# A 21st turned head, more turned steps in the MLP's middle, and output sums on ScalarE and GpSimd, in an attention and MLP kernel

## Chip, cores and metric

The kernel runs on one core of one Trainium2 chip. The metric is the device time of one execution in microseconds (us); lower is better.

## What is computed

All in float32, with S = 2048 tokens, D = 448, 16 heads of 28 columns that share one key and one value head, and F = 1792:

```python
xn  = layernorm(x)
q   = (xn @ wq) in 16 heads;  k = xn @ wk;  v = xn @ wv
att = softmax(q k^T * 28**-0.5) v, heads joined, @ wo
mlp = gelu(layernorm(xn) @ w1 + b1) @ w2 + b2
out = x + att + mlp
```

## The kernel before

Tokens are cut into 4 chunks of 512 columns (`CW`). A float32 product is made of three single-pass matmuls on a high part and a low part (`xh`, `xl`, `w1h`, `w1l` and so on). There are three stages.

**First stage (to about 65 us).** Norms, projections, `ks` (keys, all 2048 columns), `vs` (values), and queries written to DRAM as `qd`.

**MLP (about 65 to 487 us).** `slot(n)` runs one of 56 pairs (chunk, 128 rows of F): 11 matmuls of the first layer into the one bank `ph` (`mlp1`, L262 to L267), ScalarE and GpSimd work for the gelu, and 12 matmuls of the second layer for the pair of two slots earlier (`mlp2`, L787). Between those 12, `stages` calls jobs by position: `closing` and `middle` are the gelu's second and third part, `texp` is `turned_exp`. The loop over `slot(n)` (from L837) counts the matmuls: with `pace` 21, each matmul adds 21 to `owed`, and whenever a multiple of 46 is passed, one **step** of the attention's preparation is issued, 10.5 per slot. It is of one of two kinds:

- a **max step** (`max_stream`, L668 and L669): one matmul of 128 queries by 512 keys, and a VectorE reduce to the row maximum. A head takes 16. The maxima go into the score matmul as two more rows (`load_max`), so that the exp can be taken with keys on the partitions.
- a **turned step** (`turned_scores`, L704 and L705): the same matmul for a head of `TURNED`, but VectorE scales the scores into the SBUF tile `raw` and takes the maximum on the way. After four steps (one tile of 128 queries, L711 joins the four maxima) two exps of 128x1024 (`turned_exp`, L722) follow on ScalarE, and four DMAs (L725) on SP's queue store the tile in DRAM, turned by blocks. 16 steps make a head. There are two `raw` tiles (`RAWS`), and a step that finds more than two exps queued yields without work.

In a slot up to four turned steps come first (not in the odd slots of the first chunk), then max steps.

**Attention (487 us to the end).** 16 units (chunk c, group g of 4 heads), each of 16 key tiles. A **plain head** takes per key tile one score matmul with keys on the partitions (L1104) and one exp (L1105); a **turned head** has its exps in DRAM, `load_quarters` (L902 on) brings them back by 512 KB DMAs on SP's queue, two per `quarter` tile of six, each behind a one-element VectorE memset that marks the buffer as free (L912), and VectorE transposes 128x1024 of it by 32x32 blocks (`turn_blocks`, L1080). Then four matmuls of 32 columns each add the weighted values (`pv`, L1068). So 16 turned steps take the place of 16 max and 16 score matmuls.

`TURNED` lists the turned heads: head 3 of each unit, and head 2 of units 9, 11, 13 and 15; 20 in all.

The order of the attention is written out by hand: `ORDERS` has one string for each four key tiles (64 of them). `s` is a score, `m` a max step, `t` a turned step, `x` a turned exp, `T` a transpose, a digit that many key tiles of weighted values, `n` a step of the unit's normalization (`norm_jobs`: GpSimd DMAs and multiplications), `e` the next unit's maxima, `o` a step of the output product, `|` the second half. `BANKS` gives the PSUM bank (0 to 6) of each product in that order. What the MLP has not done of the 320 turned and 704 max steps is done here: 128 and 314.

`o_jobs` (L937 on) adds, for each of a chunk's four token tiles, 12 matmuls (L944 to L946) into one bank, and VectorE adds it to the row tile `a` (L948), which goes out. In the attention `loads` is GpSimd's queue, which takes the query and row-sum DMAs.

Of the kernel before, what the change touches and what calls it, by code (L numbers as in the profile page):

```python
# [26 lines left out]
SCALE = DH ** -0.5  # L27
PAIRS = 13
ORDERS = (
    "ssmsmssmmmssmTmssTs|ss",  # L30
    "tss|4TtstssmsstmsmstsssT",
    "Tsxsm|4estssmsmssmtsmsmTss",
    "ssxssTTms5smsmssmmmsms|s",
    "sstssxmTtxm3mmnmsnstTssns|ssms",
    "Tss3|stnnmssmmssmtssTsxss",
    "smT|nssxs6Teststmsmsstssnsnn",
    "TsnssT|mss3tsmsnstsmmsssmmx",
    "sTxsmsnns|s4Tmsmtsssmsnss",
    "nssnT|tsT3sstsstsmmsntsssx",
    "Tst|smsx4nnnTesmsmnsmtssssxss",  # L40
    "ssm4Tsmmssmss|nnstsmTsss",
    "|snTnsnm2ssmmsmssmsssmsmttxT3msm",
    "sstnTs|nssmmsmxT3smsmsnnntsssmm",
    "tmmsxsns|s3TstmesmtsTnssxsnss",
    "n|Tts5nxsmsssmTstmsnmsss1nss",
    "|nmstmtssTmstTsssms4omsmmomsssn",
    "sss|onnmTsmmxn3sTmemnsotssstosss",
    "mmxnT|tss3smsnmnsmmssmssmsTsnmms",
    "sxsm4xTtsnsmm|sssttstsnsxnxsTs",
    "tsnsTs6Ttmsststsossmssso|",  # L50
    "nTs2s|mssmmntsssstttssssm3To",
    "3xnxTsmss|nmsnmTmsnemsssxomsssmsm",
    "|sTssnsnsTsmontsnmmnmtxssts4smsm",
    "|ssmntTsnssTxstmxstm4mtsnsnstsms",
    "sns|xTs5nxesmnmstsssnstmsssT",
    "T|snsnomstsmssstsTttss2sns",
    "|ssmmssmmtxnnm5xTmstssmssnTsss",
    "T|sxsmottnsssmmsmsmxtm3T1msmmtsnnsss",
    "Tn|smnssse2smssmsmsnTsss",
    "sstnx|mx4nTtsmstsssnmmmsssTsns",  # L60
    "TssT3|stssnmmssssxsnss",
    "m|mx3Tstsstsnmmmmmssnm4oooooTmtssnonsmsosmsm",
    "sTn|tmmxT4xsmsmsmssmntsmststnnsss",
    "|smtsmTsm3stemsssmmmsTnmsmsmnss",
    "xTmmn4|ssmssnmmsnnsmtTsssntxsss",
    "ssT5sTTmtsmTnsnmss|s",
    "o|TTs4snsnmmsmnmTsTssmnsmx",
    "T|Tsnsss4essmstTsmTmo",
    "ssntsTsmx4TnnmTsT|sss",
    "sssnmnnmt4tnsstsxmsm|mTnmxossssmnsT",  # L70
    "ns|Toesssnmmststnsnmmntxxtmmm4mmssmmsmsmsT",
    "|ssTssmnnssmmT5mmsstsnstsms",
    "T|mssmtmomsstTsm2sntsmmssstmsxs",
    "T|mnmmT5msmnTTsstnsssss",
    "Tn4sTmssnm|TnsmsnTsss",
    "TTsxs4men|sssnsssTT",
    "sTsnTssTx51snTm|msmss",
    "mmssmsxnmssTssmnn2mnmsmsTstssn|",
    "ss1ssm|tsmnssmttTttsxoxmt4esoosnnmssmmT",
    "ssonssmtT|sn3smmnssmssmnnmTss",  # L80
    "xossxTsmomTt5mos|msnmssmnmsmssss",
    "|sTmTsnTs3msntostsnToss",
    "smsmmnsTTtsnsTsn6|Tss",
    "TstmsnmtnTostsxmsTe7Txnmssm|ts",
    "Tnnssmnosmsmn|TmxxnttTsTosss",
    "s|TTst6tsmmmsnnssmxmsss2sss",
    "TmtststTssts3xnnxmmsssmsmnnmsxsm|s",
    "ssTs3ensnsTssns|ssss",
    "sT3s|nssssTssssn3sns",
    "Ts|snssssT2nnTssT",  # L90
    "TsTsTss2ssnn|Tss",
    "ssss2TsTsooso4TsoT|",
    "sssTssssT|s3TT",
)
BANKS = (
    "0163240516324053126543126043512604352106342510634251063425016324051632450163245013465201345620135640"
    "2135640213546023150426314502631450236451203645102364150236145023641502346510324653102465301425603145"
    "2063145206345120163452061345260314526031456230145632104562314056234105623401526354021635410256431025"
    "6431026540635142063510462504635120641325063412506342105634251064235106425316042530416523041562031465"
    "2103465210346521304652130465132064532104653210463045621340526314052631450264352106435210463521046352"  # L100
    "1064532106453126045132604513624015362453016243501264350126435012645031642501346250143560214365021436"
    "5021436510423651402635401263540126345012506342156043201456320146503421650342165304261354601235406213"
    "5402615324103416520431650234160523416052431605431260541302564325160425361402610523460512346051234061"
    "5342016532401635204165302416530246153206543120643512046351024631052460351420653210465231046532106532"
    "4106532406513245061324506132405163025461302564130526134052164350216043521604351260435612045361240356"
    "1203456102435604132560143520641352601453601245631024651302465132046513204635104635210462315046231506"
    "42351604325610345216304521630452163045216304521630452130452130452130415230415"
)
TURNED = tuple((u, j) for u in range(16) for j in ((3, 2) if u in (9, 11, 13, 15) else (3,)))
RAWS = 2  # L110
GELU = 0.044715, 0.7978845608028654
KEPT = 1, 2, 3
MLP_ORDER = 1, 2, 3, 0
# [5 lines left out]
def block_kernel(ctx, tc, x, wq, wk, wv, wo, w1, b1, w2, b2, out):  # L119
# [4 lines left out]
    def f(t):  # L124
        return t.bitcast(F32)
# [569 lines left out]

    def turned_scores(i):
        for t in range(CT):
            while len(exps) > 2:
                yield
            raw = keep.tile([P, 4, 4, P], F32, name="raw", bufs=RAWS)  # L700
            m3 = keep.tile([P, 8], F32, name="m3", bufs=RAWS)
            for n in range(4):
                sc = mtile([P, CW])
                pe.matmul(sc, q3[i % 2][:, t * P:(t + 1) * P], ks[:, n * CW:(n + 1) * CW], start=True, stop=True)  # L704
                dve.tensor_scalar(raw[:, n].rearrange("p r (b i) -> p b r i", i=32),  # L705
                                  sc.rearrange("p (b r i) -> p b r i", r=4, i=32), SCALE, -3e38,
                                  op0=ALU.mult, op1=ALU.max, accum_out=m3[:, n:n + 1])
                if (t, n) == (0, 3) and 0 < i < len(TURNED) - 1:
                    load_m(*TURNED[i + 1], q3[1 - i % 2])
                if n == 3:  # L710
                    dve.tensor_reduce(m3[:, 4:5], m3[:, 0:4], axis=AX.X, op=ALU.max, negate=True)  # L711
                    exps.extend((TURNED[i], t, raw, m3, h) for h in range(2))
                yield

    stored = {}

    def turned_exp():
        if not exps:
# [23 lines left out]
    def split(c, ft):  # L742
        return c == 0 and ft % 2 == 1
# [53 lines left out]
    def slot(n):  # L797
        nonlocal maxed, ending, later_low
        middle = high = low = none
        closing, ending = ending, none  # L800
        if n < len(mslots):
            if n == 0:
                high, later_low = w2_split(0)
            if n > 1 and split(*mslots[n]):
                high, low = w2_split(n // 2)
                high()
            middle, ending = yield from mlp1(*mslots[n], closing if n == 1 else none)
        if n == 2:
            later_low()
        texp = turned_exp if n < len(mslots) - 1 else none  # L810
        stages = {0: texp, 1: texp, 2: low, 3: closing, 5: middle}
        if n == 0:
            stages = {0: middle, 1: high}
        if n == 1:
            stages = {1: texp, 2: texp, 3: middle}
        if n == 3:
            stages = {0: closing, 1: low, 2: texp, 3: texp, 5: middle}
        if n in norms:
            stages = {4: norms[n], 5: texp, 6: texp, 7: closing, 8: norms[n], 9: middle, 10: low}
        if n >= 2:  # L820
# [16 lines left out]
    for n in range(len(mslots) + 2):  # L837
# [22 lines left out]
        if c == NCH - 1 and 6 <= ft < 12:  # L860
            for i in (2 * ft - 12, 2 * ft - 11):
                q, r = divmod(i, 4)
                nc.sync.dma_start(ahead[q][:, 4 * r:4 * r + 4, :], td[0, 3][q, :, 4 * r:4 * r + 4])
        ts, pace = 0, 21
        if n == 2:
            pace = 20
# [35 lines left out]
    def load_quarters(n):  # L902
        u, q = divmod(n // 2, 4)
        at = slice(8 * (n % 2), 8 * (n % 2) + 8)
        for j in (3, 2):
# [6 lines left out]
            dve.memset(part[0:1, 0, 0:1], 0.0)  # L912
            nc.sync.dma_start(part, td[u, j][q, :, at])

    pool.memset(wor, 0.0)
# [21 lines left out]
    def o_jobs(c, gs, tiles=range(CT)):  # L937
        last = NG - 1 in gs
        for k in tiles:
# [5 lines left out]
                pe.matmul(po, oth[:, ts], wol[:, g, :], start=False, stop=False)  # L945
                pe.matmul(po, otl[:, ts], woh[:, g, :], start=False, stop=(g == gs[-1]))  # L946
            a = rows[c, k]
            dve.tensor_add(a, a, po)  # L948
            if last:
                nc.sync.dma_start(ov[:, CT * c + k, :], a)  # L950
            yield
# [254 lines left out]
```

## Time and profile before

| | us |
|---|---|
| median of 3 runs | 1047.93 |
| lowest, highest | 1047.56, 1048.78 |
| the profiled execution | 1048.25 |
| its span, first to last instruction | 1046.4 |
| MLP up to | about 487 |
| attention from there | about 559 |

The profile is of one execution. Engines are PE (TensorE's matmuls), PEld (its weight loads), DVE (VectorE), ACT (ScalarE), POOL (GpSimd) and SP (SyncE's queue). A row of the timeline has start, length, engine, line and operation; neighbouring equal operations are joined with their count, so the length of a joined row spans all of them. A group row of the page has busy time, mean ns of one, and the idle time before with what ended it. A window row has, for each engine, the busy time and the number of instructions, then the granted clock of TensorE, the DMA engines' share and GB/s. A row of waits has total, number of times and the longest.

### The profile page before, as it was taken

What the parts mean: (1) busy time and instruction counts of PE and PEld (TensorE: products, weight loads), DVE (VectorE), ACT (ScalarE), POOL (GpSimd) and SP (SyncE); (2) the same over time, 40 slices, a digit from 0 to 9 for tenths busy, and PEclk for the clock granted to TensorE, in tenths of its full rate; (3) what the DMA queues carried; (4) which work ended last, traced back from release to release, by engine and by line L of the source; (5) the groups of instructions that cost most, each with busy time, mean ns of one, the idle gap of its engine ahead of it and who ended that gap; (6) DMA issues with size and microseconds to landing.
All of it is one profiled execution on the core that took longest, in us unless ns stands there. A gap on an engine that the chain in (4) does not pass through costs nothing.

```text
span 1046.4 us, 17964 instructions
## 1 busy us (share of the span) xinstructions
PE 1037.4 (99%) x5757; PEld 704.9 (67%) x5757; DVE 935.1 (89%) x1998; ACT 722.8 (69%) x1216; POOL 562.0 (54%) x704
## 2 busy tenths in 40 slices
PE   8999999999999999999999999999999999999998
PEld 8778888888888888886555545655555555455555
DVE  7889999999999999999887988878899999998956
ACT  6765555565566565655899888877877666875892
POOL 6679787678766777875244354234335342441230
PEclk9999999999999999999999999999999999999999
DMA  8866455767776867984789798887889998899892
GB/s 273 252 212 168 120 141 146 186 153 196 194 190 157 205 174 192 265 231 137 217 247 263 219 270 231 254 252 241 245 241 267 308 258 287 269 292 308 265 354 78
DMA packets 234130, 234.33 MB, mean 224 GB/s; under 512 B 19007, under 2 KB 199373, under 8 KB 234037
## 3 DMA queue, kind: packets, MB, share of 16 engines
q1 hardware_dynamic: 221684, 212.45, 69.8%
q0 software_dynamic: 10944, 20.17, 7.5%
q8 instruction: 45, 0.74, 0.3%
q10 hardware_dynamic: 1408, 0.57, 0.2%
q14 instruction: 49, 0.39, 0.1%
HBM read 133.21 MB, written 98.68 MB: 222 GB/s over the span
## 4 chain that ended last, share of the span: by engine, by line
PE 91%; DVE 4%; DMA 3%; issue 1%; ACT 1%; ACTq 0%; DVEq 0%
PE po L1068 19%; PE m L1104 15%; PE m L668 15%; PE m L787 12%; PE ph L262 11%; PE m L704 7%; PE qp L262 3%; DMA quarter<-td 2%; DVE mx L669 2%; PE ph L265 1%; PE ph L267 1%; PE m L944 1%; PE m L946 1%; PE m L945 1%; DVE p L1080 1%
## 5 line engine op out<-in xcount | busy, mean ns | idle before, releaser
L669 DVE TENSOR_REDUCE mx<-m 128x1 f32<-128x512 f32 x704 | 451.8, 682 | 32.3 <-PE m L668 29.7
L1105 ACT ACTIVATE p<-m 128x512 f32<-128x512 f32 x612 | 318.1, 633 | 79.8 <-PE m L1104 78.2
L668 PE MATMUL m<-ks,qm 128*128 128x512 f32 x704 | 268.6, 399 | 1.6 <-DVE mx L669 0.6
L705 DVE TENSOR_SCALAR_CACHE_REDUCE raw<-m 128x512 f32<-128x512 f32 x320 | 212.3, 684 | 22.0 <-PE m L704 18.3
L1104 PE MATMUL m<-xh,ks 128*128 128x512 f32 x704 | 223.6, 406 | 0.0
L1068 PE MATMUL po<-p,vs 128*32 128x512 f32 x1664 | 221.0, 595 | 0.4 <-DVE p L1080 0.4
L722 ACT ACTIVATE raw<-raw,m 128x1024 f32<-128x1024 f32 x160 | 180.1, 1165 | 4.4 <-DVE m L711 4.2
L1104 PEld LDWEIGHTS m<-xh,ks 128*128 128x128 f32 x704 | 127.6, 188 | 68.4 <-issue 15.9
L1080 DVE STREAM_TRANSPOSE p<-quarter 128x1024 f32<-128x1024 f32 x133 | 161.1, 1228 | 7.6 <-DMA quarter<-td 7.2
L668 PEld LDWEIGHTS m<-ks,qm 128*128 128x128 f32 x704 | 131.4, 188 | 45.6 <-issue 7.5
L752 ACT ACTIVATE hx<-ph,b1t 128x512 f32<-128x512 f32 x55 | 37.9, 690 | 150.1 <-PE ph L267 98.7
L1068 PEld LDWEIGHTS po<-p,vs 128*32 128x32 f32 x1664 | 55.6, 109 | 109.2 <-issue 103.1
L704 PE MATMUL m<-ks,q 128*128 128x512 f32 x320 | 125.5, 399 | 0.0
L768 POOL TENSOR_TENSOR hl<-hx,hh 128x512 fp32r<-128x512 f32 x56 | 72.5, 1294 | 32.7 <-ACT hh L766 32.7
L787 PE MATMUL m<-w2h,hl 128*128 128x448 f32 x224 | 81.4, 367 | 0.0
L787 PE MATMUL m<-w2h,hh 128*128 128x448 f32 x224 | 81.3, 366 | 0.0
L787 PE MATMUL m<-w2l,hh 128*128 128x448 f32 x224 | 81.2, 366 | 0.0
L756 POOL TENSOR_TENSOR hz<-hz,hx 128x512 f32<-128x512 f32 x56 | 72.8, 1299 | 4.6
L761 POOL TENSOR_TENSOR hx<-hx,hz 128x512 f32<-128x512 f32 x56 | 72.6, 1297 | 4.7
L704 PEld LDWEIGHTS m<-ks,q 128*128 128x128 f32 x320 | 59.8, 188 | 22.2 <-issue 5.0
L633 POOL DMA_DIRECT2D xh<-qd x60 | 37.5, 626 | 64.7 <-PE m L668 40.8
L1068 PE MATMUL po<-xh,vs 128*32 128x512 f32 x256 | 68.2, 596 | 0.0
(198 smaller groups left out, 1529.6 us busy)
## 6 DMA issues: line engine op xcount, KB each, us to landing
td<-raw SPq DMA_DIRECT2D x320, 256.0 KB
quarter<-td SPq DMA_DIRECT2D x154, 512.0 KB
xh<-qd POOLq DMA_DIRECT2D x44, 168.0 KB, 5.4
qd<-qe SPq DMA_DIRECT2D x24, 256.0 KB
a<-in_A_x_dram SPq DMA_DIRECT2D x24, 224.0 KB
qm<-qd SPq DMA_DIRECT2D x96, 56.0 KB
qm<-qd POOLq DMA_DIRECT2D x80, 56.0 KB, 5.4
ad<-a SPq DMA_DIRECT2D x16, 224.0 KB
```

The lines of the kernel that those rows point to most:

```text
L262: pe.matmul(ps, w, v, start=(n == 0), stop=False)
L668: pe.matmul(pm, qm[:, t * P:(t + 1) * P], ks[:, n * CW:(n + 1) * CW], start=True, stop=True)
L669: dve.tensor_reduce(mx[:, CT * j + t, n:n + 1], pm, axis=AX.X, op=ALU.max)
L704: pe.matmul(sc, q3[i % 2][:, t * P:(t + 1) * P], ks[:, n * CW:(n + 1) * CW], start=True, stop=True)
L705: dve.tensor_scalar(raw[:, n].rearrange("p r (b i) -> p b r i", i=32), sc.rearrange("p (b r i) -> p b r i", r=4, i=32), SCALE, -3e38, op0= ...
L722: act.activation(raw[:, rs], raw[:, rs], AF.Exp, bias=m3[:, 4:5], scale=1.0)
L756: pool.tensor_mul(hz, hz, hx)
L787: pe.matmul(m2[k], h[:, k * P:(k + 1) * P], w[:, ft, :], start=(ft == 0 and i == 0), stop=(ft == NF - 1 and i == 2))
L1068: pe.matmul(po[32 * j:32 * j + 32, :], vs[:, kt, :], ps.pop((u, kt, j)), start=(kt == 0), stop=(kt == NT - 1))
L1080: dve.transpose(p.rearrange("p k (g j) -> p g k j", j=32), part[:, :, 32 * k:32 * k + 64].rearrange("p g (k j) -> p g k j", j=32))
L1104: pe.matmul(s, ks[:, kt * P:(kt + 1) * P], qss[u][:, j, :], start=True, stop=True)
L1105: act.activation(p, s, AF.Exp, scale=SCALE)
```

## The change

- `TURNED`: the second turned head is in units 4, 7, 10, 13 and 15 now; 21 turned heads. `ORDERS` and `BANKS` are written anew for it.
- `MORE = 15, 43`: from slot 15 to slot 43 a third tile for `raw` is taken from the pool `xl_p`; in these slots up to 4, 8, 4 turned steps (by n % 3) come first, up to four exps may be queued, and `mlp2` has two more places (7 and 9) for a turned exp.
- `load_quarters`: the memset only ahead of the first half of a `quarter` tile.
- `o_jobs`: for chunks 0 to 2 ScalarE copies the bank to a new tile `ot` (one buffer), and GpSimd adds it to `a`. The last chunk's sums stay on VectorE.

In the order strings the letters now count: `s` 688 (704 before), `m` 334 (314), `t` 108 (128), `x` 54 (64), `T` 168 (160); weighted sums 254 key tiles in both.

```diff
-TURNED = tuple((u, j) for u in range(16) for j in ((3, 2) if u in (9, 11, 13, 15) else (3,)))
+TURNED = tuple((u, j) for u in range(16) for j in ((3, 2) if u in (4, 7, 10, 13, 15) else (3,)))
 RAWS = 2
+MORE = 15, 43
...
     def turned_scores(i):
         for t in range(CT):
-            while len(exps) > 2:
+            while len(exps) > (4 if third else 2):
                 yield
-            raw = keep.tile([P, 4, 4, P], F32, name="raw", bufs=RAWS)
-            m3 = keep.tile([P, 8], F32, name="m3", bufs=RAWS)
+            turn_of[0] = (turn_of[0] + 1) % 3 if third else 0
+            raw = third[0] if turn_of[0] == 2 else keep.tile([P, 4, 4, P], F32, name="raw", bufs=RAWS)
+            m3 = keep.tile([P, 8], F32, name="m3", bufs=RAWS + 1)
...
-    stored = {}
+    stored, third, turn_of = {}, [], [0]
...
+        if MORE[0] <= n < MORE[1] + 2:
+            for i in (7,9):
+                if i not in stages:
+                    stages[i] = texp
...
+        if n == MORE[0]:
+            third.append(f(xl_p.tile([P, 4, CW], F32R, name="xl")).rearrange("p a (b k) -> p a b k", k=P))
+        if n == MORE[1]:
+            third.clear()
...
+                elif third and ts < (4, 8, 4)[n % 3]:
+                    ts += tq.step()
+                elif third:
+                    maxed += mxs.step()
                 elif ts < 4 and n < len(mslots) - 1 and not split(c, ft):
...
-            dve.memset(part[0:1, 0, 0:1], 0.0)
+            if n % 2 == 0:
+                dve.memset(part[0:1, 0, 0:1], 0.0)
             nc.sync.dma_start(part, td[u, j][q, :, at])
...
             a = rows[c, k]
-            dve.tensor_add(a, a, po)
+            if c < NCH - 1:
+                t = att.tile([P, D], F32, name="ot", bufs=1)
+                act.activation(t, po, AF.Copy)
+                pool.tensor_add(a, a, t)
+            else:
+                dve.tensor_add(a, a, po)
```

Of `ORDERS` every string is new; the 43rd, in unit 10, for one:

```diff
-    "|ssTssmnnssmmT5mmsstsnstsms",
+    "nTmmmsnmnsns4|txTmssmmsostoTTmsn",
```

More of the change, by code (lines that the diff above doesn't have):

```diff
@@ L29 @@
 ORDERS = (
[L30 to L70, printed above, removed]
@@ L71 @@
-    "ns|Toesssnmmststnsnmmntxxtmmm4mmssmmsmsmsT",
-    "|ssTssmnnssmmT5mmsstsnstsms",
[L73 to L93, printed above, removed]
+    "ssmmssmmsmsTmsT|sssss",
+    "|sTs3stsmmsmsssmTtsttsss",
+    "s3esmsmssttms|stTsmxxsmsss4Tm",
+    "sst|sssmTTsxxstssms4tsttsm",
+    "sssssxsmsmm2TmsmtssmnsT|ns",
+    "ssstsns3|mesnnstsmssxsmTTs",
+    "sssTss|4msnstssnxxstssT",
@@ new lines @@
+    "sm5Tsmsstsmnnttss|mssssTs",
+    "sTs2smsnstsmnmsnmsssmssT|",
+    "ssTsn|2mtmssxsnsnsmTmsn2esstns",
+    "nmmtsss|nmssxm23TxnmsmnsmssnmxTsss",
+    "Tsssns4|ssTmssmssmsmns",
+    "ss|Tnnt5Tmnsnmsmnsmsssssss",
+    "|TTmn2mmssmsmmnssssmsnssnnss",
+    "T2n|ttsmsttstTtemnx4xmstsssmsmmsmsss",
+    "snTm|tmxts2mssssnntmssssmsTs",
+    "T|s6snnTTTmsmssmxsss",
+    "TTTsstnT4|1nesmsnmsmsmsnms",
+    "snsmmtTTxsss3nssT|Ts",
+    "sossTssTxT4mssmns|T",
+    "ss1mtssnnmnsmss|smssmtntT3motomsmnTsmn",
@@ new lines @@
+    "TssssntmT5mstsnsmsmm|sssns",
+    "mmnmmos|nsmmxtex2smsmssmnmsmnnsmTsnssTnsm",
+    "sxstxms32TtsmmssstssstnTomo|xomss",
+    "m4|nsommsmssssmstxTostsmsmttsmsT",
+    "ssom|msssmsmnTssTmmsxxt5stsms",
+    "|msmtsnnsmTsstntm4enmnsssmsxTmsss",
+    "Tsmomsmtsmsmnn|mssTsm3nstmssmss",
+    "|TnTomsssmmnTnstmx4Tmsnmnmsmsmns",
+    "|TsnTsTsTexn5ssmtsnssm",
+    "TsmssnmsnnTsmTn|3ssTs",
+    "ss|nTssTxsmTs6Tss",
+    "mss|sstnmssTssmn2smnmnmssTs",
+    "smsmnn2otsm|stssttnsmTTssmsxmssx",
+    "T|snsnTe5smsssmsnomstmtmxmxtm3tossmsmsm",
@@ new lines @@
+    "ssmstssmTtmmsTx|s4ssmsnsmnmsnm",
+    "Tsnmxnsms2tttossmsssnsnsTmtsm2n|s",
+    "|msmsmsnmsomsnmssmmnTsossTss",
+    "s|Tsse5xmssmnsmsssmsstsxnnT",
+    "mmsT3osmsmssnmsmntsmsmstsstm|mnnsT",
+    "soT6Tn|mtmsmstTsnmsomsmmTsst",
+    "TsmTsxssnsx|T4sesTs",
+    "nTmmmsnmnsns4|txTmssmmsostoTTmsn",
+    "ssssxTssTsmT42nntTst|",
+    "s|ssTsssomssnmmsnstmsmmsnT",
+    "ssxs2mms|mssnnnmtsnxmtsmmT5stesnmtTss",
+    "|ssssTTssnsn4msmnsmssmnms",
+    "ssttsxmssmsxn|nmsTT4snmssmmsms",
+    "mssmssssntTmmmst3mtmsssn|mssnoTm",
@@ L94 @@
+    "osmTs|4xxmestssmmsotstssTsnss",
+    "ssnTsms3nno|msnssmssonmxssTts",
+    "3smstsmsnmssnsmmnmsmsTT|sossm",
+    "Tsmmnmn6nosnmmtomsmxm|nmmonssnmsTsTmnnsT",
+    "TssTsomts|4tnstTsnssT",
+    "xsTmt|em4ssmtTsTmsxsmTss",
+    "noxTsTsmsTmss6nmnn|smmTmss",
+    "|sssmss2sTnnmmmxssssnTosnmmms",
+    "TmsTssmssnss6smssnmmsn|ms",
+    "sssmsmmsmsms3TsesnssTs|",
+    "ss3ssssssTssTnnssn3|",
+    "s|sTnnsssssT2nnsTT",
+    "Tssnss|sTT2ssnTs",
+    "ssss2Toso6TTsssT|",
+    "sssosssoTssT1T2|T",
 )
@@ L95 @@
 BANKS = (
[L96 to L105, printed above, removed]
@@ L106 @@
-    "1203456102435604132560143520641352601453601245631024651302465132046513204635104635210462315046231506"
-    "42351604325610345216304521630452163045216304521630452130452130452130415230415"
+    "0163240516234102546102534610253640125342563401256340123546102354610235460125304612534012653146502341"
+    "5602341056234105623415062341506324105463210546325140326514032651403621540362154032163540216354023156"
+    "4230156420315642031564201354602135462013546201356421035641023654102364501623450162345102643150264301"
@@ new lines @@
+    "5624310562143056123460512346051234650214635021463502146352014635210463521405632140625430621543026154"
+    "3206145361204536102543601532640132564013265401352641035624103546021354602143052164350261345012634501"
+    "2360415326041523640152364015234610354621034562103546120354621304526130452631045231645023164502316450"
+    "2341560231465032146053214650324510625134065231460253146025314602531460253415602341562034512630425610"
+    "3425613042561340521640315624031562403156243061524306152430612534620512304651342503614250631204631520"
@@ L108 @@
+    "4624631502643105264301526453012653041265304162534025136402531642051364205134260513426051324601532406"
+    "1250346125036421035462310254631054263104652310645213650241365021436520134265013426053146203456120435"
+    "6102463510264315024316503246105324610352413654103265132406514306521340562134056213064210654231065432"
+    "0165340216530421653042165304216530421530421530421534021534021"
 )
-TURNED = tuple((u, j) for u in range(16) for j in ((3, 2) if u in (9, 11, 13, 15) else (3,)))
+TURNED = tuple((u, j) for u in range(16) for j in ((3, 2) if u in (4, 7, 10, 13, 15) else (3,)))
```

## The prediction, made before the changed kernel was run

> **What bounds the kernel now.** I read the page's busy times first, then its chain of work, then the busy times by stage, then single stretches of the timeline.
>
> ```profile
> PE 1037.4 (99%) x5757; PEld 704.9 (67%) x5757; DVE 935.1 (89%) x1998; ACT 722.8 (69%) x1216; POOL 562.0 (54%) x704
> ...
> PE 91%; DVE 4%; DMA 3%; issue 1%; ACT 1%; ACTq 0%; DVEq 0%
> ```
>
> The chain that ended last lies on PE for 91%, with DVE at 4% and DMA at 3%. A busy PE row alone proves little, because matmul ends are modelled, so the next view takes the two long stages apart: the MLP's middle, and the attention.
>
> ```profile
> core 0: us, PE busy (x) PEld busy (x) DVE busy (x) ACT busy (x) POOL busy (x), PEclk, DMA share, GB/s
> 175.00:425.00 250.00, 249.56 (x1132) 209.72 (x1131) 237.91 (x541) 149.89 (x207) 181.74 (x178) 1.00 0.72 185
> 485.00:1034.00 549.00, 548.24 (x3424) 296.37 (x3426) 476.60 (x984) 433.42 (x797) 199.75 (x319) 1.00 0.86 257
> ```
>
> In the MLP's middle DVE is busy for 237.9 of 250 us, so it has 12.1 us free; ACT has 100 us free. In the attention DVE has 72 us free, ACT 116, POOL 349. The clock is 1.00 throughout. Whether PE really has no holes is read from the distance between starts:
>
> ```profile
> 299.65 0.36 PE L787 MATMUL m<-w2h,hl 128*128 128x448 f32 x1
> 299.85 0.40 PE L668 MATMUL m<-ks,qm 128*128 128x512 f32 x1
> 300.09 0.39 PE L262 MATMUL ph<-xh,w1h 128*128 128x512 f32 x1
> ...
> 300.78 0.39 PE L704 MATMUL m<-ks,q 128*128 128x512 f32 x1
> 301.00 0.39 PE L262 MATMUL ph<-xh,w1h 128*128 128x512 f32 x1
> ```
> ```profile
> 566.43 0.40 PE L1104 MATMUL m<-xh,ks 128*128 128x512 f32 x1
> 566.67 0.39 PE L668 MATMUL m<-ks,qm 128*128 128x512 f32 x1
> 566.89 0.40 PE L1104 MATMUL m<-xh,ks 128*128 128x512 f32 x1
> 567.13 0.39 PE L668 MATMUL m<-ks,qm 128*128 128x512 f32 x1
> 567.36 0.39 PE L704 MATMUL m<-ks,q 128*128 128x512 f32 x1
> 567.59 2.06 PE L1104 MATMUL m<-xh,ks 128*128 128x512 f32 x8
> ```
>
> A 512-column matmul starts 0.22 to 0.24 us after the one ahead of it, in both stages, whichever of the three lines it comes from (score L1104, max L668, turned L704). From 566.43 to 567.59 five take 1.16 us: **0.23 us each**. One of 448 columns takes 0.20 (L787). In both stages they follow each other at this spacing, so I take PE's instruction list as the bound: one matmul less is 0.23 us less.
>
> **The change part by part.** *The 21st turned head* (unit 4, 7 and 10 get a second one, 9 and 11 lose theirs). A plain head costs 16 max matmuls and 16 score matmuls; a turned one costs 16 turned matmuls. So over the run 16 of L1104 go (704 to 688), 16 of L668 go (704 to 688), 16 of L704 come (320 to 336). Net: 16 matmuls fewer, **16 x 0.23 = 3.7 us** off PE, on the path.
>
> The Trainium skill, "TensorE: Matmul & The Clock Gate", section "Back-to-back issue gap", gives 131 ns per matmul of 512 columns as a sustained stream, and about 216 ns for an isolated one. By its 131 ns the 16 would be worth 2.1 us and the sum below would be -1.7; the trace's starts, 0.22 to 0.24 us apart, do not agree with that figure.
>
> *What is moved.* The letters of the order strings count as: turned steps `t` 128 to 108, max steps `m` 314 to 334, scores `s` 704 to 688, exps `x` 64 to 54, transposes `T` 160 to 168. So 36 turned steps enter the MLP and 36 max steps leave it. On PE that is an even exchange in each stage (rows above: L668 and L704 cost the same). Groups of weighted sums that stand together without a matmul of another kind between them: 70 before, 70 after, so PE's switching between the two kinds costs nothing new. DVE next:
>
> ```profile
> 250.50 0.69 DVE L705 TENSOR_SCALAR_CACHE_REDUCE raw<-m 128x512 f32<-128x512 f32 x1
> 251.12 0.08 DVE L705 DVE_READ_ACCUMULATOR raw<-m 128x1 f32 x1
> 251.18 0.69 DVE L705 TENSOR_SCALAR_CACHE_REDUCE raw<-m 128x512 f32<-128x512 f32 x1
> ...
> 251.92 0.16 DVE L711 TENSOR_REDUCE m<-m 128x1 f32<-128x4 f32 x1
> 251.99 2.06 DVE L669 TENSOR_REDUCE mx<-m 128x1 f32<-128x512 f32 x3
> ```
> ```profile
> 261.28 2.47 DVE L669 TENSOR_REDUCE mx<-m 128x1 f32<-128x512 f32 x4
> ```
>
> Turned steps follow each other at 0.68 us, and the fourth, with the reduce of four maxima, takes 251.99 - 251.18 = 0.81. Max steps back to back take (2.47 - 0.68) / 3 = 0.60. A turned step is thus dearer by 0.08 + 0.13 / 4 = 0.11 us, and 36 of them put **4.0 us more on DVE in the MLP's middle**. What hides it is the 12.1 us that DVE has free there. Without that cover it would cost its 4.0. A step's lag must fit into three PSUM banks; a slot of eight turned steps needs 8 x 0.71 + 2.5 x 0.60 = 7.2 us of DVE, against 21.5 x 0.23 + 12 x 0.20 = 7.3 us of PE (11 matmuls of the first layer, 12 of the second, 10.5 steps). I take 0.4 us, a tenth of the price, and keep 0 and 4.0 as ends.
>
> ```profile
> L1105 ACT ACTIVATE p<-m 128x512 f32<-128x512 f32 x612 | 318.1, 633 | 79.8 <-PE m L1104 78.2
> ...
> L722 ACT ACTIVATE raw<-raw,m 128x1024 f32<-128x1024 f32 x160 | 180.1, 1165 | 4.4 <-DVE m L711 4.2
> L1080 DVE STREAM_TRANSPOSE p<-quarter 128x1024 f32<-128x1024 f32 x133 | 161.1, 1228 | 7.6 <-DMA quarter<-td 7.2
> ...
> L846 POOL TENSOR_TENSOR a<-a,b2b 128x448 f32<-128x448 f32 x13 | 15.0, 1158 | 0.0
> ...
> L948 DVE TENSOR_TENSOR a<-a,m 128x448 f32<-128x448 f32 x16 | 9.7, 608 | 6.6 <-PE m L946 6.4
> ...
> L960 ACT ACTIVATE oc<-po 128x512 f32<-128x512 f32 x15 | 9.2, 616 | 22.2 <-issue 19.0 <-POOL otl L991 3.2
> ...
> L912 DVE MEMSET quarter<- 1x1 f32 x154 | 6.6, 59 | 0.1
> ```
>
> ACT in the MLP: 18 exps more x 1.17 = 21 us over 30 slots, at the new stages 7 and 9. They stand after the tanh, where ACT now waits:
>
> ```profile
> 259.43 0.69 ACT L752 ACTIVATE hx<-ph,b1t 128x512 f32<-128x512 f32 x1 [2.88 <-POOL hx L761]
> ```
>
> Two exps (2.3 us) fit into that idle 2.88; if they ran over, the `ph` bank would be freed later, while the second layer's 12 matmuls and their steps are still in hand. Cost 0. The third raw tile keeps a tile's reuse about two slots away, as two tiles at one per slot do now.
>
> *Attention, sums.* DVE: -20 turned x 0.71 + 20 max x 0.60 + 8 transposes x 1.23 - 73 marker memsets x 0.06 (half of 162 loads keep theirs) - 12 output adds x 0.61 = -14.2 + 12.0 + 9.8 - 4.4 - 7.3 = **-4.1 us**. ACT: -16 exps x 0.63 - 10 x 1.17 + 12 copies of 128x448, not in the trace, between 0 and 0.62 (L960, wider; taken) = -10.1 - 11.7 + 7.4 = **-14 us**. POOL: +12 adds x 1.16 = +14 us, beside 349 free. None of these is on the chain, so each counts 0 on the time. They could thin out the small waits of weight loads for banks:
>
> ```profile
> PEld m L1104 <- ACT p L1105: 13.5, 43, 0.8
> ...
> PEld m L668 <- ACT p L1105: 5.2, 22, 0.8
> ```
>
> Of these 18.7 us most is hidden behind the running matmul; a tenth less would be 1.9 us. I take 0, with -1.9 as an end. Behind an ACT copy stand the exps of the next scores, with seven banks of room; behind a POOL add stand query loads that are due a unit later, and the shares of the row sums.
>
> *DMA.*
>
> ```profile
> td<-raw SPq DMA_DIRECT2D x320, 256.0 KB
> quarter<-td SPq DMA_DIRECT2D x154, 512.0 KB
> ```
> ```profile
> 425.00:450.00 25.00, 25.00 (x116) 21.37 (x115) 23.77 (x55) 14.84 (x21) 19.80 (x20) 1.00 0.99 288
> ```
>
> Nine tiles of four 256 KB stores go into the MLP's middle: 9.4 MB over some 210 us, 45 GB/s on top of 185, when 288 GB/s have been moved at a share of 0.99. The share there would go from 0.72 to about 0.9. In the attention five tiles of stores go (-5.2 MB) and eight loads come (+4.2 MB). Cost 0, with the rival below. On SP the stores stand in order with the loads of the next max head; these are due a dozen steps later, and max steps come more rarely there. A second-half load without its memset only waits for its buffer, no longer for DVE's place in its order: earlier, never later.
>
> *Sum.* -3.7 + 0.4 = -3.3 us. The profiled execution took 1048.25 us (span 1046.4, 1.85 around it), which is 0.32 above the median of the runs. So 1044.95 in its terms, and **1044.6 us** against the median of 1047.93. A change of 0.2% (2.1 us) is about what a measurement tells from none.
>
> **The rivals.**
>
> *DVE sets the pace.* By busy share (237.9 of 250, 95%) DVE is close to full in the MLP, and the third bank could be what PE waits for. Then the MLP grows by the whole 4.0 us, and PE's 3.7 in the attention are given back: 1047.93 - 3.7 + 4.0 = 1048.2. Against it speaks PE's even spacing. The skill's "Perfetto Trace Analysis", section "Identifying the Most-Contended Engine", speaks for it: matmul busy time is a bad measure and the weight loads' share a better one, which is 296 of 549 us here, 54%, in the attention, while DVE has 87%. By that rule the attention would go with DVE's sum, -4.1, and the MLP with +4.0: again about 1047.8. In this trace the weight loads of the 32-wide weighted sums are short and leave PE full all the same. Chance 0.12.
>
> *The transfers come late.* Double heads stand in units 4 and 7, where scores are otherwise full, and a raw tile can wait for its store.
>
> ```profile
> DVE p L1080 <- DMA quarter<-td: 7.2, 4, 4.1
> ...
> POOL ld L976 <- DVE rc L975: 54.6, 9, 14.5
> ```
>
> DVE waited for a quarter four times, 4.1 us at longest. One such longest wait more on the chain gives 1044.6 + 4.1 = 1048.7; half of one 1046.6. For it: a share of 0.86 on average in the attention. Against it: 1 MB less there in all. Chance 0.12.
>
> *Slower: POOL holds the sum's only buffer.* The tile `ot` has one buffer. In unit 10 two sums of chunk 1 stand with one score and one turned step between them ("ostoT"). The second ACT copy must wait until POOL has added the first, and POOL's queue is in order: before, it stood still for up to 14.5 us for a reciprocal. Then ACT stops, exps with it, and PE after the second sum's 12 matmuls (2.8 us) and seven banks (1.6): 14.5 - 4.4 = 10.1 us, 1044.6 + 10.1 = **1054.7**. It makes the kernel slower by over 0.2% once such a wait exceeds 3.3 + 2.1 + 4.4 = 9.8 us. Against it: nine waits in 549 us, and the other sums stand well apart. Chance 0.10.
>
> **How the numbers follow.** The forecast has 0.66, with a range of its own from 1042.3 (waits thin out by 1.9, MLP costs nothing) to 1046.2 (the MLP costs 2.0, half of its price). The two middle rivals have 0.24, the slower one 0.10. Leaving out that one and little else, the range is 1042.0 to 1048.9. Faster: nearly all of the forecast, 0.65. Same: the middle rivals and the forecast's upper edge, 0.25. Slower: 0.10.
>
> **What would show it.** Right: L1104 x688, L668 x688, L704 x336, starts still 0.23 apart in both stages; the MLP's end no later than before by over 0.5 us; the attention shorter by 3 to 4 us; DVE's busy time up by about 4 us in the MLP and down by as much behind it. Wrong: PE holes behind DVE or a raw store between 175 and 425 us (first rival); long waits of L1080 for a quarter in units 4 and 7 (second); the ACT copy waiting for POOL in unit 10 (third). A gain far over 3.7 us would mean that PE had waits that I did not see.

## The result: slower, and the profile after

| | before | after |
|---|---|---|
| median (4 runs each) | 1048.14 us | **1052.88 us** |
| lowest, highest | 1047.56, 1048.78 | 1052.60, 1055.61 |
| the profiled execution, its span | 1048.25, 1046.4 | 1052.6, 1050.8 |

The ratio is 1.0048, 95% interval 1.0036 to 1.0061: slower by 4.7 us where 3.3 us less were forecast. The miss is 8 us, and the time lies outside the range, on the side that had the chance of 0.10.

First the page of the kernel after: busy times, and the chain that ended last.

```profile
PE 1040.8 (99%) x5741; PEld 704.0 (67%) x5741; DVE 938.4 (89%) x1941; ACT 726.1 (69%) x1220; POOL 576.3 (55%) x716
...
PE po L1088 18%; PE m L669 15%; PE m L1124 14%; PE m L789 12%; PE ph L263 11%; PE m L706 7%; PE qp L263 3%; DMA tr<-ld 1%; PE m L959 1%; PE ph L266 1%; DMA td<-raw 1%; PE ph L268 1%; PE m L961 1%; PE m L960 1%; PE po L1071 1%
```

PE has 16 matmuls fewer (5741 for 5757) and is busy 3.4 us *longer*. So part of the loss isn't idle time; matmuls have become longer. The chain's line names two transfers that it did not name before, `tr<-ld` (row sums) and `td<-raw` (a turned tile's store). The groups show that the program does what the change says:

```profile
L669 PE MATMUL m<-ks,qm 128*128 128x512 f32 x688 | 267.2, 402 | 1.7 <-DVE a L794 0.7
L1124 PE MATMUL m<-xh,ks 128*128 128x512 f32 x688 | 221.5, 406 | 0.8 <-DVE raw L707 0.7
...
L706 PE MATMUL m<-ks,q 128*128 128x512 f32 x336 | 133.0, 404 | 0.9 <-DVE raw L707 0.7
```

Scores 688, max steps 688, turned steps 336, as counted. Next, where the time goes: the first and the last second-layer matmul of the MLP, in the timelines of the kernel before and the kernel after.

```profile
73.80 0.36 PE L787 MATMUL m<-w2h,hh 128*128 128x448 f32 x1
...
480.64 0.36 PE L787 MATMUL m<-w2h,hl 128*128 128x448 f32 x1
```
```profile
73.76 0.37 PE L789 MATMUL m<-w2h,hh 128*128 128x448 f32 x1
...
485.01 0.37 PE L789 MATMUL m<-w2h,hl 128*128 128x448 f32 x1
```

I call the distance between these two starts the MLP, and the rest of the span behind the second the attention. The MLP went from 406.8 to 411.2 us (+4.4); the attention took 1046.4 - 480.64 = 565.8 before and 1050.8 - 485.01 = 565.8 after. So the MLP lost 4.4 us and the attention did not gain its 3.7. The waits of ScalarE for the copy of the weighted sums (`oc`), before and then after, are the first lead for the attention:

```profile
ACT oc L960 <- POOL otl L991: 3.2, 2, 2.3
```
```profile
ACT oc L980 <- POOL otl L1011: 13.4, 7, 5.8
ACT ot L965 <- PE m L961: 10.6, 11, 1.9
```

By this view the copy for the new sums (`ot`, second row of after) only ever waits for PE, never for POOL. The older copy `oc<-po` (L980), which the change doesn't touch, waits for POOL seven times and up to 5.8 us, where it had waited twice and 2.3 at most.

### The profile page after: what moved, and what is told of

Read it like the earlier page. It is cut to its first block, busy times and chain, and to the rows that moved or that the text cites. A ratio compares the mean times of both kernels' runs of the same rounds, so it can differ in the third digit from the quotient of the medians.

```text
span 1050.8 us, 17890 instructions
## 1 busy us (share of the span) xinstructions
PE 1040.8 (99%) x5741; PEld 704.0 (67%) x5741; DVE 938.4 (89%) x1941; ACT 726.1 (69%) x1220; POOL 576.3 (55%) x716
## 4 chain that ended last, share of the span: by engine, by line
PE 90%; DMA 3%; ACT 1%; POOL 1%; DVE 1%; issue 1%; SPq 0%; ACTq 0%; DVEq 0%; POOLq 0%
PE po L1088 18%; PE m L669 15%; PE m L1124 14%; PE m L789 12%; PE ph L263 11%; PE m L706 7%; PE qp L263 3%; DMA tr<-ld 1%; PE m L959 1%; PE ph L266 1%; DMA td<-raw 1%; PE ph L268 1%; PE m L961 1%; PE m L960 1%; PE po L1071 1%
## 5 line engine op out<-in xcount | busy, mean ns | idle before, releaser
L670 DVE TENSOR_REDUCE mx<-m 128x1 f32<-128x512 f32 x688 | 441.2, 682 | 37.0 <-PE m L669 34.0
L1125 ACT ACTIVATE p<-m 128x512 f32<-128x512 f32 x598 | 311.8, 628 | 70.7 <-PE m L1124 69.1
L669 PE MATMUL m<-ks,qm 128*128 128x512 f32 x688 | 267.2, 402 | 1.7 <-DVE a L794 0.7
L707 DVE TENSOR_SCALAR_CACHE_REDUCE raw<-m 128x512 f32<-128x512 f32 x288 | 192.0, 686 | 25.4 <-PE m L706 15.9
L1100 DVE STREAM_TRANSPOSE p<-quarter 128x1024 f32<-128x1024 f32 x141 | 169.1, 1224 | 2.5 <-PE po L1088 1.9
L724 ACT ACTIVATE raw<-raw,m 128x1024 f32<-128x1024 f32 x144 | 161.2, 1160 | 6.9 <-DVE m L713 6.9
L669 PEld LDWEIGHTS m<-ks,qm 128*128 128x128 f32 x688 | 128.6, 188 | 49.2 <-issue 10.9
L706 PE MATMUL m<-ks,q 128*128 128x512 f32 x336 | 133.0, 404 | 0.9 <-DVE raw L707 0.7
L706 PEld LDWEIGHTS m<-ks,q 128*128 128x128 f32 x336 | 62.9, 188 | 25.5 <-issue 5.0
L1088 PE MATMUL po<-xh,vs 128*32 128x512 f32 x256 | 73.1, 596 | 0.0
L756 POOL TENSOR_SCALAR hz<-hz 128x512 f32<-128x512 f32 x56 | 35.0, 625 | 59.5 <-ACT hz L755 59.3
```

Of the source, the lines that this page charges most:

```text
L669: pe.matmul(pm, qm[:, t * P:(t + 1) * P], ks[:, n * CW:(n + 1) * CW], start=True, stop=True)
L670: dve.tensor_reduce(mx[:, CT * j + t, n:n + 1], pm, axis=AX.X, op=ALU.max)
L724: act.activation(raw[:, rs], raw[:, rs], AF.Exp, bias=m3[:, 4:5], scale=1.0)
L1088: pe.matmul(po[32 * j:32 * j + 32, :], vs[:, kt, :], ps.pop((u, kt, j)), start=(kt == 0), stop=(kt == NT - 1))
L1100: dve.transpose(p.rearrange("p k (g j) -> p g k j", j=32), part[:, :, 32 * k:32 * k + 64].rearrange("p g (k j) -> p g k j", j=32))
L1125: act.activation(p, s, AF.Exp, scale=SCALE)
```

## The experiments

The theory at the start: the third `m3` buffer moves every tile behind it, and their new places make matmuls longer. Its rivals: the added turned steps fill VectorE in the MLP's middle (the prediction's first rival); the new order of the attention, or the sums' new way, brings waits there; the memset that half of the loads lost had kept them from running ahead. Where a ratio is given, it is against the kernel before in runs on the same chip; "MLP" and "attention" are of the profiled execution.

### Only the places move

To the kernel before (`e1_shift`):

```diff
-            m3 = keep.tile([P, 8], F32, name="m3", bufs=RAWS)
+            m3 = keep.tile([P, 8], F32, name="m3", bufs=RAWS + 1)
```

Two tiles are used as before, in turn of three; eight float32 more per partition, 32 bytes, push everything behind. In the program before, `xh`, `w1h` and `w2h` start at bytes 39040, 98688 and 179072 of a partition, all multiples of 64; now, as in the kernel after, they start 32 bytes later.

> The kernel before with one edit: a third buffer of m3 (32 bytes per partition), which no work needs; every SBUF tile behind m3 moves up by 32 bytes, as in the changed kernel. Theory 'layout' (512-column matmuls start 0.230 to 0.234 us apart in the changed kernel's MLP, 0.227 in the kernel before, from the first slots on, where the programs do the same): 1050 to 1052 us, with the MLP about 2 us longer and the attention 1 to 2 us longer, and the starts at 0.23 to 0.234. Theory 'MLP middle' (waits behind the 36 added turned steps) and theory 'output sums' (ACT and POOL coupled by one buffer): 1048.1, no change within 0.3 us.

Measured: 1050.46 (11 runs) against 1047.87, ratio 1.0029 (1.0016 to 1.0042). Nothing of the order or the work is changed. To find which tiles, `e12_wp32` puts the 32 bytes further back, ahead of the MLP's weights and gelu tiles, so that keys, queries and `xh` stay; `e11_shift64` takes one buffer more than `e1_shift`, 64 bytes in all. Both start from the kernel before; the first diff is that of `e12_wp32`:

```diff
+    wp.tile([P, 8], F32, name="gap")
```
```diff
-            m3 = keep.tile([P, 8], F32, name="m3", bufs=RAWS)
+            m3 = keep.tile([P, 8], F32, name="m3", bufs=RAWS + 2)
```

> The kernel before with a spare tile of 32 bytes at the start of the pool wp: the first layer's weights and all tiles of the MLP behind them (gelu tiles, second layer's weights) 32 bytes up, but not the turned input xh and xl, the query tiles, or any tile of the attention. If the MLP's own operands cause the slower starts: the MLP 2 us or more longer, 1050 us. If xh, xl or the query tiles do: as before, 1047.9.

> The kernel before with two spare buffers of m3 instead of one: all later tiles 64 bytes up. Theory 'places at a multiple of 64 bytes': as before, 1047.9 within 0.6 us, MLP's 512-column starts at 0.227. Rival 'any other place, or more m3 buffers': as e1_shift, 1050.5.

`e12_wp32`: 1051.55 against 1047.89, ratio 1.0030 (1.0021 to 1.0039). `e11_shift64`: 1048.79 against 1047.89, ratio 1.0009 (1.0000 to 1.0018). The groups of PE between 85 and 478 us (busy us, then mean ns of one): the kernel before, then `e1_shift`, `e12_wp32`, `e11_shift64`.

```profile
L668 PE MATMUL m<-ks,qm 128*128 128x512 f32 x370 | 145.9, 394 | 0.4
L787 PE MATMUL m<-w2h,hl 128*128 128x448 f32 x215 | 78.5, 367 | 0.0
...
L704 PE MATMUL m<-ks,q 128*128 128x512 f32 x184 | 72.5, 394 | 0.0
L262 PE MATMUL ph<-xh,w1h 128*128 128x512 f32 x156 | 61.2, 392 | 0.0
```
```profile
L668 PE MATMUL m<-ks,qm 128*128 128x512 f32 x365 | 144.9, 397 | 0.3
...
L704 PE MATMUL m<-ks,q 128*128 128x512 f32 x184 | 73.6, 400 | 0.0
L262 PE MATMUL ph<-xh,w1h 128*128 128x512 f32 x156 | 61.4, 394 | 0.0
```
```profile
L669 PE MATMUL m<-ks,qm 128*128 128x512 f32 x365 | 144.9, 397 | 0.3
...
L705 PE MATMUL m<-ks,q 128*128 128x512 f32 x184 | 73.3, 398 | 0.0
```
```profile
L668 PE MATMUL m<-ks,qm 128*128 128x512 f32 x370 | 146.5, 396 | 0.4
L787 PE MATMUL m<-w2h,hl 128*128 128x448 f32 x214 | 77.4, 362 | 0.0
```

The reader is to see 2 to 6 ns on one matmul of 512 columns, whichever line it comes from. No wait goes with it: idle time before L668 (L669) is 0.3 or 0.4 us in each. It adds up over the MLP, whose last second-layer matmul stands at 480.64 before and here in `e1_shift` and `e12_wp32`:

```profile
73.82 0.37 PE L787 MATMUL m<-w2h,hh 128*128 128x448 f32 x1
...
483.22 0.37 PE L787 MATMUL m<-w2h,hl 128*128 128x448 f32 x1
```
```profile
74.41 0.36 PE L788 MATMUL m<-w2h,hh 128*128 128x448 f32 x1
...
484.13 0.37 PE L788 MATMUL m<-w2h,hl 128*128 128x448 f32 x1
```

MLP 409.4 and 409.7, for 406.8: **2.6 to 2.9 us for 32 bytes** (2.0 to 2.3 against 407.4, the longest of three profiles with the old MLP in its old places). With 64 bytes it is 407.0, and the whole time, 1048.79, lies between the two that were expected: matmuls of 512 columns are longer there too, but those of 448 are shorter by 5 ns. The attention does not grow (565.8 before, then 564.9, 564.4, 565.1). In `e12_wp32` the operands of L669 stand where they stood, and it is slower all the same; so it isn't a matmul's own operands alone. Which tile it is, and by what path, these runs do not tell.

### The change with its tiles left in place

`e2_exact`: the kernel after, with the third `m3` in the unused rest of the tile `one`, so that all other tiles but `tr2` and the new `ot` keep their old places.

```diff
-    one = keep.tile([P, 3], F32, name="one")
+    one = keep.tile([P, 8], F32, name="one")
...
-            m3 = keep.tile([P, 8], F32, name="m3", bufs=RAWS + 1)
+            m3 = one[:, 3:8] if turn_of[0] == 2 else keep.tile([P, 8], F32, name="m3", bufs=RAWS)
```

> The changed kernel with its third m3 placed in the unused rest of the tile 'one', so that every SBUF tile of the MLP and of the attention but tr2 and ot lies where it lay before the change. Theory 'layout': 1052.9 - 3.5 = 1049 to 1050 us, starts of 512-column matmuls back at 0.227 us in the MLP. Theories 'MLP middle' and 'output sums': 1052.9 within 0.5 us.

1049.00 (12 runs) against 1047.87, ratio 1.0011 (1.0001 to 1.0022). The next two were run together on another chip: the same kernel again, `e6_exact2`, and the kernel after unchanged, `e5_after`.

> The changed kernel with the old places of all tiles (as e2_exact) a second time, beside the changed kernel. Theory 'layout': 2.5 us (the MLP's difference in e1_shift) to 3.9 us faster than e5_after. What is left above before's time less 3.7 us is then due to waits: 1.5 us in the MLP, and the rest in the attention, to be read from this second profile.

> The changed kernel itself again, beside the other three on one chip. All theories: slower than before by 4 to 5 us (1.004 to 1.005), with 512-column starts at 0.233 us in the MLP.

`e6_exact2` 1049.61, ratio 1.0010 (1.0000 to 1.0020); `e5_after` 1051.73, ratio 1.0042 (1.0028 to 1.0055), against 1047.93. Places are worth 1051.73 - 1049.61 = **2.1 us** of the change by the medians, and 0.0032 of 1048, 3.4 us, by the ratios. The kernel is still not faster than before.

### Parts of the change on their own

`e7_mlponly`: the kernel before with the third raw tile and the 36 more turned steps in the MLP (tiles in place as in `e2_exact`), still 20 turned heads; in `ORDERS` of before the first 36 `t` become `m` and the first 18 `x` go (the second string, for one).

```diff
-    "tss|4TtstssmsstmsmstsssT",
+    "mss|4TmsmssmssmmsmsmsssT",
```

> The kernel before with the MLP's middle of the change alone (third raw tile, 36 more turned steps, exps at places 7 and 9), old places of all tiles, the first 36 turned steps and 18 exps of the attention's order taken out and 36 max steps put in; 20 turned heads, so PE has the same work as before. Theory 'MLP middle': the MLP 1.5 to 2.5 us longer, the attention as before: +1.5 to +2.5 us. If the lighter attention (4 us of VectorE, 21 us of ScalarE less) shortens waits for banks: +0 or below.

1049.18 (12 runs) against 1047.93, ratio 1.0005 (0.9993 to 1.0018): no difference that can be told. Its MLP took 408.2 us.

`e8_sumsonly`: the kernel before, only with the output sums of chunks 0 to 2 through ScalarE and GpSimd.

```diff
-            dve.tensor_add(a, a, po)
+            if c < NCH - 1:
+                t = att.tile([P, D], F32, name="ot", bufs=1)
+                act.activation(t, po, AF.Copy)
+                pool.tensor_add(a, a, t)
+            else:
+                dve.tensor_add(a, a, po)
```

> The kernel before with the output sums of three chunks through ScalarE and GpSimd alone. Theory 'VectorE's sums cost time' (e3_dvesums was some 6 us longer in the attention than the other variants): -1 to -4 us. Theory 'only the written order decides' (the change's order counts on a free VectorE at those places, the old one does not): within 0.5 us of before.

1048.29 (12 runs) against 1047.93, ratio 1.0005 (0.9994 to 1.0015). In the old order the sums may be done on either side.

`e3_dvesums`: the kernel after with all sums on VectorE again.

```diff
-            if c < NCH - 1:
-                t = att.tile([P, D], F32, name="ot", bufs=1)
-                act.activation(t, po, AF.Copy)
-                pool.tensor_add(a, a, t)
-            else:
-                dve.tensor_add(a, a, po)
+            dve.tensor_add(a, a, po)
```

> The changed kernel with VectorE adding the output sums of all chunks again, without the tile ot. Theory 'output sums' (the ACT copy delays score exps, POOL stands waiting for it): 1050 to 1051 us, the attention 2 to 3 us shorter. Theories 'layout' and 'MLP middle': 1052.9, or up to 0.5 us more because VectorE has 7 us of work more.

1059.24 (5 runs) against 1047.87, ratio 1.0108 (1.0092 to 1.0123): some 6.3 us *worse* than the kernel after (1.0108 - 1.0048 = 0.0060 of 1048), which none of the expectations had. In the new order the same twelve additions cost what they had not cost in the old.

`e4_memsets`: the kernel after with the memset ahead of both halves again.

```diff
-            if n % 2 == 0:
-                dve.memset(part[0:1, 0, 0:1], 0.0)
+            dve.memset(part[0:1, 0, 0:1], 0.0)
```

> The changed kernel with a marker memset ahead of both halves of a quarter tile again, as before. If loads that start early take DMA bandwidth from stores and row loads: 1 to 2 us faster. Theories 'layout', 'MLP middle' and 'output sums': 1052.9 within 0.5 us (4 us more of VectorE, hidden).

1050.91 (8 runs), ratio 1.0031 (1.0021 to 1.0042), which overlaps with that of the kernel after. So far the lost memsets are not shown to cost time or to save any.

### The buffer ahead of ScalarE's copy

What was left in `e6_exact2` was read from its profile. Its waits of PE and of ScalarE in the attention (total, times, longest):

```profile
PE m L669 <- ACT p L1125: 3.3, 2, 1.9
```
```profile
ACT oc L980 <- POOL otl L1011: 16.0, 7, 7.4
```

And the chain of waits from 553 to 561 us, ahead of the first of PE's two stops:

```profile
546.47 7.79 DMA tr<-ld
...
554.43 1.29 POOL oc L1004
...
557.69 1.29 POOL otl L1011
...
559.00 0.05 ACT oc L980
...
559.50 0.60 ACT p L1125
560.14 0.50 PE m L669
```

Read from above: the row sums' transfer takes 7.79 us (8.47 ahead of the second stop); POOL can multiply only then, and makes `oth` and `otl` from the product; between product and `oth` it issues two query loads, 1.23 us. `oc` has one buffer. So the *next* unit's copy stands in ScalarE's queue until `otl` is done, the exps stand behind it, PE finds no free bank and stops. The experiment is one number (`e9_oc2`, on top of `e6_exact2`; the second place that allots `oc` likewise):

```diff
-        oc = att.tile([P, CW], F32, name="oc", bufs=1)
+        oc = att.tile([P, CW], F32, name="oc", bufs=2)
```

> The changed kernel with the old places of the tiles (as e2_exact, 1049.0 to 1049.6 us) and with two buffers for oc, the copy of a unit's weighted sums. Theory 'row-sum chain': in the new order ScalarE's copy of the next unit stands 11 to 16 us in all behind GpSimd's last read of the one oc, which waits for the row sums' DMA (3 to 5 us in the old order); score exps stand behind it. With two buffers this wait is gone: 1045 to 1047.5 us, the copy's wait for GpSimd under 2 us in all. Rival 'fewer scores just leave other waits' (VectorE, banks): 1049 within 0.5 us.

> The kernel before with two buffers for oc alone. Theory 'row-sum chain': the old order has 3 us of this wait, none of it at a PE stop: 1047.9 within 0.6 us. Rival 'the second buffer helps any order': 2 us or more faster.

`e9_oc2`: **1046.54** (12 runs, 1044.65 to 1047.97) against 1047.89, ratio 0.9981 (0.9972 to 0.9991). It beats both kernels. The old order does not need the buffer: `e10_before_oc2` 1047.33, ratio 0.9993 (0.9984 to 1.0001). The buffer also moves `oth`, `otl`, `rc` and `tr` by 2048 bytes, in both kernels alike, so their new places are not what helped. ScalarE's waits in `e9_oc2`:

```profile
ACT oc L980 <- POOL oth L1010: 4.7, 1, 4.7
ACT oc L980 <- POOL otl L1011: 2.9, 1, 2.9
```

Two waits of 7.6 us in all for seven of 16.0; PE's row behind `ACT p` is gone. One pair of profiles would not carry this: in `e2_exact`, the same program as `e6_exact2`, such waits were 11.1 us and PE stood only 0.2 us behind `ACT p`. The effect rests on the 12 runs of each kernel, each set against before on its own chip.

### The two small edits again, without that wait

`e13_oc2_memsets` is `e9_oc2` with the edit of `e4_memsets`, `e14_oc2_dvesums` is `e9_oc2` with the edit of `e3_dvesums`.

> The mended kernel (e9_oc2, 1046.5 us) with a marker memset ahead of both halves of a quarter tile again. Theory 'early second halves crowd the row sums' DMAs': 1 to 2 us faster, 1044.5 to 1045.5. Rival 'the halved memsets cost and gain nothing': 1046.5 within 0.6 us.

> The mended kernel (e9_oc2, 1046.5 us) with VectorE adding all output sums again. If the 7 us more in e3_dvesums came through VectorE alone: 1051 us or more. If they came through the copy oc that the order made late (which is mended here): within 1 us of 1046.5.

`e13_oc2_memsets` 1046.71 (12 runs) against 1048.45, ratio 0.9988 (0.9974 to 1.0002): memsets cost nothing that shows. `e14_oc2_dvesums` 1052.15 (5 runs), ratio 1.0043 (1.0030 to 1.0056). `e9_oc2` did not run on this chip, so `e13_oc2_memsets` stands in for it: the sums' way is worth 1052.15 - 1046.71 = **5.4 us** in the new order (6.5 by the ratios of `e14_oc2_dvesums` and `e9_oc2`). PE's waits in `e14_oc2_dvesums` point at VectorE, and the chain ahead of the first of the two stops (the one of 1.8 us) shows the addition, two transposes and a max reduce one behind the other before PE goes on:

```profile
PE m L1119 <- DVE quarter L927: 1.8, 1, 1.8
PE m L1119 <- DVE a L963: 1.3, 1, 1.3
```
```profile
853.05 0.26 DVE a L963
...
853.59 2.37 DVE p L1095 x2
855.96 0.57 DVE mx L670
...
856.59 0.50 PE m L1119
```

These two stops are 3.1 of 5.4 us; the rest I did not trace to its waits.

## Why the prediction was wrong, by its own steps

Taken from the runs on one chip and then, on another, from `e9_oc2`: +3.8 (`e5_after`, 1051.73 - 1047.93) falls to +1.7 with the tiles in place and to -1.35 with two `oc` buffers (1046.54 - 1047.89), where -3.3 was forecast. By the ratios it is +4.4, +1.0 and -2.0. Two steps of the prediction failed, the fixed spacing and the copies on ScalarE; the first costs 2.1 to 3.4 us, the second 3.0.

- **"16 x 0.23 = 3.7 us off PE, on the path": right in kind, its size not settled.** The matmuls went as counted. The attention of `e2_exact` and `e9_oc2` took 1043.7 - 481.70 = 562.0 and 1042.9 - 480.59 = 562.3 us. Six profiles in the old order with sums on VectorE (before, `e1_shift`, `e7_mlponly`, `e10_before_oc2`, `e11_shift64`, `e12_wp32`) took 564.3 to 565.8, 564.8 on average. So 2.6 us or so, up to 3.8 against the highest. But the two profiles are of executions 3.5 and 1.9 us under their kernels' medians: they show what the new order takes when PE hardly stops (0.5 and 0.6 us), not what it takes as a rule. The 131 ns of the Trainium skill ("TensorE: Matmul & The Clock Gate", "Back-to-back issue gap"), which the prediction weighed, would have given 2.1 us. The starts in the trace speak for 0.23 a matmul; the scatter of the stage is too wide to tell the two apart by the total.
- **"In both stages they follow each other at this spacing, so I take PE's instruction list as the bound": the spacing itself was taken as fixed, and this step failed for 2.1 to 3.4 us.** `bufs=RAWS + 1` stood in the diff, and the prediction did not price it at all. The Trainium skill, "SBUF — State Buffer", section "Operand start alignment", lets a float32 operand start at any multiple of its element size and says that this is about legality and that its runs timed nothing. Here 32 bytes made the MLP longer by 2.6 and 2.9 us of 406.8, twice, with no wait added.
- **MLP's middle, "I take 0.4": small, 0.8 measured.** The MLP of the six kernels with added turned steps and tiles in place (`e2_exact`, `e6_exact2`, `e7_mlponly`, `e9_oc2`, `e13_oc2_memsets`, `e14_oc2_dvesums`) took 407.2 to 408.7, 407.9 on average; of those with the old MLP in old places or 64 bytes on (before, `e8_sumsonly`, `e10_before_oc2`, `e11_shift64`) 406.8 to 407.4, 407.1 on average. The first rival's 4.0 did not come, though the MLP did grow by 4.4: without `e1_shift` it would have passed for that rival. (Four profiles with added steps and moved tiles, after, `e3_dvesums`, `e4_memsets` and `e5_after`, took 409.8 to 411.2, 410.6 on average; 407.1, the 0.8 and 2.6 or 2.9 for the places come to 410.5 or 410.8.) Nor did VectorE's busy time there rise by the 4.0 that the prediction priced and named as a sign: between 175 and 425 us it was 237.91 before, 235.77 after and 237.50 in `e9_oc2`. Why the dearer steps do not show in it stays open. The third raw tile was not always in time; in the kernel after, 175 to 430 us:

```profile
DVE raw L707 <- DMA td<-raw: 3.1, 2, 1.6
```

- **"Behind an ACT copy stand the exps of the next scores, with seven banks of room": this step failed for 3.0 us**, 1.7 + 1.35. The sentence was about the new copies of `ot`. The copy that held the exps was `oc<-po`, moved against its releaser by the new `ORDERS`; the prediction counted the letters of the strings and did not follow the chain copy, row sums, `otl`, next copy through them. The wait stood in its own view (L960, 3.2 us for `otl`). Nor did it ask how long `tr<-ld` takes.
- **The third rival, "POOL holds the sum's only buffer": right shape, wrong buffer.** Its chance was for `ot`, which never waited for POOL; a single buffer on ScalarE, held by POOL, did decide. (Its 2.8 us for 12 matmuls of 448 columns are at 0.23 each; at the 0.20 that the prediction read for this width they are 2.4.)
- **The sums on VectorE, "None of these is on the chain, so each counts 0 on the time": it holds with the move, and would not have held without it.** The prediction gave the move no worth beyond 7.3 us of work on an engine with 72 us free. Without it the new order is 5.4 to 6.3 us worse, in the old order it makes no difference. The free 72 us are an average; where `o`, `m` and `T` stand close together, as in the chain of `e14_oc2_dvesums` above, there are none.
- **The second rival, quarters too late in units 4 and 7: did not come.** VectorE's transposes waited less than before (7.6 us idle then, mostly for a quarter), and for PE:

```profile
L1100 DVE STREAM_TRANSPOSE p<-quarter 128x1024 f32<-128x1024 f32 x141 | 169.1, 1224 | 2.5 <-PE po L1088 1.9
```

- **Memsets, DMA share, PE's switching: 0 was right** as far as the runs can tell; the share in the middle came to 0.85, where about 0.9 was estimated:

```profile
175.00:425.00 250.00, 248.78 (x1116) 206.21 (x1115) 235.77 (x579) 167.03 (x223) 179.20 (x175) 1.00 0.85 221
```

What stays open: the last 2.0 us, between `e9_oc2`'s median (-1.35) and -3.3; 1.3 by its ratio. Its profiled execution took 1044.66 and has a single wait of PE in the attention; most of its runs took longer, up to 1047.97.

```profile
PE m L1124 <- DVE raw L707: 0.6, 1, 0.6
```

The profiled execution of `e13_oc2_memsets` was a long one, 1051.37, and PE's and VectorE's waits in its attention are:

```profile
PE m L1123 <- DVE raw L707: 3.4, 2, 1.8
PE m L706 <- DVE raw L707: 0.7, 1, 0.7
```
```profile
DVE raw L707 <- DMA td<-raw: 5.7, 3, 2.2
```

There two raw tiles are all there are, and a late store reaches PE. The longest of these stops, 1.84 us, ends at 743.42, and right behind it the clock granted to TensorE is about half for 3.4 us:

```profile
743.80:747.20 3.40, 3.40 (x13) 1.26 (x15) 3.40 (x6) 1.68 (x3) 0.56 (x1) 0.51 0.98 377
```

Two more profiles show such a stretch, `e8_sumsonly` behind a stop of 2.93 us and `e3_dvesums` behind one of 1.71. In that of `e8_sumsonly` matmuls of 448 columns start 0.37 us apart, and 0.20 right behind it; by these two a stretch of 3.4 us loses some 1.5 us (an estimate), nearly as much as the stop of 1.84 itself. Length alone does not decide: stops of 1.8 us in `e14_oc2_dvesums`, 1.85 in `e6_exact2` and 1.6 here had no such stretch behind them. Three of the 12 executions of `e13_oc2_memsets` have a mean granted clock of 0.998, as this one has, and took 1049.26 to 1051.37; the nine others have 1.00 and took 1045.31 to 1048.23. That late stores, with the clock behind them, make up the 2.0 us of `e9_oc2` is argued, not shown: one of its 12 executions has 0.998, and a third raw tile in the attention was not tried.

## What to carry to other kernels

Before pricing an edit by its instructions, ask what it does to the *places* of all tiles behind it, and try a kernel that has the new places and the old work: here it alone showed 2.6 of the 4.7 us. A stop of PE can cost more than its length: behind one of 1.84 us the halved clock took some 1.5 us more, by the estimate above. When a hand-written order is made anew, follow each single-buffered tile from its writer round to its next writer, with the longest transfer between them, on the queues that run in order; counting letters finds the work, not the waits. An engine's free time holds for the stage as an average, and is no cover at the place where its jobs bunch.

## What had not been expected of the hardware

- 32 bytes of shift, from starts at multiples of 64 to starts between them, cost 2 to 6 ns on a 512-column matmul (392 to 394 ns before, 394 to 400 then, as recorded) and 2.6 to 2.9 us of an MLP of 406.8; 64 bytes made 448-column matmuls 5 ns shorter (367 to 362) and those of L668 2 ns longer (394 to 396); the MLP took 407.0.
- The small transfer of row sums, four rows read back from DRAM, took 7.79 and 8.47 us ahead of the two stops in one profile (`e6_exact2`), longer than any other link of the chains that stopped PE.
- Two executions of the same program, on two chips, differ by 5.4 us in the attention: 562.0 in `e2_exact` and 1049.8 - 482.4 = 567.4 us in `e6_exact2`. PE's waits there are 0.5 and 4.5 us. A single profile of either would have told a wrong tale.
- Stops of PE of 1.71, 1.84 and 2.93 us were each followed by 3.4 us at half the granted clock; others of 1.6 to 1.85 us were not.
